# A Mamba-2 + SwiGLU kernel: a new order of its later steps, outputs multiplied in two steps, powers in two passes, the last output bank in two, and four value tiles of block 0 multiplied in three parts

## The chip, the cores and the metric

The kernel runs on one core of one Trainium2 chip. The metric is the device time of one execution in microseconds (us), lower is better. The kernel before has three timed executions: a median of 369.09 us, from 368.76 to 369.15. A separate execution was profiled; it has a time of its own, given below.

A core has a matrix engine (PE in the profile, its weight loads listed apart as PEld), a vector engine (DVE), a scalar engine (ACT), a fourth general engine (POOL) and SP, which here only issues DMA transfers. Each engine works through its own list of instructions in the order of that list and stops at an instruction whose operands are not ready.

## The reference

Two blocks follow each other. The first is a Mamba-2 scan over 4 sequences of 768 tokens with 8 heads of 32 columns and a state of 16; the second is a SwiGLU feed-forward on 3072 tokens of 256 columns, with 1536 hidden columns and an RMS norm ahead of it. All of it is fp32.

```python
# scan, per chunk, batch and head
cum = cumsum(log(a)); L = exp(cum[i] - cum[j]) * causal
M = (C @ B.T) * L
y = M @ x + (C @ state) * exp(cum)
state = exp(sum(log a)) * state + sum_j B_j x_j exp(cum[-1] - cum_j)
# feed-forward on y, as 3072 x 256
xn = y / sqrt(mean(y*y) + 1e-6) * rms_g
g = xn @ w_gate;  val = xn @ w_val
out = (g * sigmoid(g) * val) @ w_out
```

## The kernel before

**Tiling.** Tokens are cut into 12 pairs `p` of 256 tokens for the scan (inside it chunks of 64 tokens) and 6 blocks `blk` of 512 tokens for the feed-forward: block `blk` is made of pairs `2*blk` and `2*blk+1`. The 1536 hidden columns are 12 tiles `f` of 128. For each block and tile there are two products of 512 tokens by 128 columns into a PSUM bank `gv`, gate (`m` = 0) and value (`m` = 1); silu of the gate (ACT, `silu.blk.f`) times the value (DVE, `hid.blk.f`) gives the hidden tile `hx`; and two output products with the out weights add it into the two banks `o` of the block.

**Two ways of multiplying.** A product of fp32 is made in one of two ways. Whole: two plain fp32 matmuls (`F`, `gv_whole`, L1140; `OF`, `o_whole`, L1203). The profile lists each of the two as two records. Split: the operand and the weights are first taken apart into three rounded parts (high, low, mixed) by ACT, DVE and POOL, and six matmuls of the fast rounded type are made, part by part (`X`, `gv_split`, L1150; `OX`, `o_split`, L1197, three matmuls of 512 columns an output bank; in block 5 the same through L1203 as six matmuls of 256 columns). The parts of the normed input `xn` come from steps `xH`/`xHv`, `xL`, `xK`; those of the weights from `wH`/`wHv`, `wL`, `wM`; those of the hidden tile from `hH`/`hHv`, `hL`/`hLp`, `hK`. The names in the profile are `xh`, `xl`, `xk`, `wh`, `wp`, `hh`, `hl`, `hk`. Which way a tile goes is a table: in block 0 tiles 0 and 1 are made early, from unnormed input; tiles 2 to 7 go whole for both gate and value (`GV4`); all else is split. Block 0's outputs all go whole (`O4`).

**Weights.** They arrive as bit words in 18 pieces `k` (two for tiles 0 and 1; 2 to 11 one gate or value half for two tiles each; 12 to 17 the out weights). Each piece is rebuilt on the chip: `pow.k` makes the powers of two on ACT (`power`, three passes over 128x512, L281 to L285, tile `e`), `man.k` the mantissas on DVE (L301), `wt.k` joins them on DVE (L307), and then the three parts follow.

**The scan** of a pair: loads by SP, differences of decays (`spread`, `sub`), exponentials on ACT (`ex`), transposes on DVE (`Tt`, `Td`), additions to the state as products of 64x32 tiles (`A`, L831), the states (`S`, DVE), products of C and B for a block (`gb`, L766), their decays (`L`, DVE), and then the outputs `y.p` (`outputs`, L916): 12 or 16 products of states with `T` and 32 products of chunks with `L`, on 32x64 and 64x32 tiles of PE. They go into four banks for a block; squares (`sq`) and copies (`yt`) by ACT empty them; means (`ms`), roots (`rs`), a broadcast by DMA (`rb`) and `xn` follow.

**The order.** All of it runs under a manual schedule: a string `order` (L1357 on) names 1177 steps, and a loop (L1483) calls each step's function in this order. Each engine's list is the instructions of these steps in that order, so a step moved in the string is moved on every engine that it uses. PSUM has eight banks; `gv`, `o`, `y` and `g` tiles take them in turn, and a bank that is asked for again waits until its last reader is done. ACT's function tables are loaded by hand through `functions` (L259): L264 for silu, L266 for exponentials and logarithms.

**The end.** After the last output products, bank 0 of block 5 is copied by DVE (`putv.5.0`) and bank 1 by ACT (`put.5.1`, L1233), each as one copy of 128x512 followed by two transfers of 128x256 from SP (L1236).

Of the kernel before, what the change touches and what calls it, by code (L numbers as in the profile page):

```python
# [50 lines left out]
def kernel(  # L51
# [222 lines left out]
    def power(k):  # L274
# [15 lines left out]
    def uses_whole(k):  # L290

        if k < 2:
            return 2
        f = 2 * (k // 2) if k < 12 else 2 * (k - 12)
        return sum((gv_mode(blk, g) == 4) if k < 12 else 2 * ((blk, g) in O4)
                   for g in (f, f + 1) for blk in range(NBLK))
# [70 lines left out]
    kinks = const.tile([P, 3], FP32, name="kinks")  # L367
# [60 lines left out]
    def kinks_of_powers():  # L428
        for k, v in enumerate((1152.0, 256.0, -1792.0 * 128.0)):
# [439 lines left out]
    yts, sqs = {}, {}  # L869
# [37 lines left out]
    def outputs(p):  # L907

        n, blk = p % 2, p // 2
        if n == 0:  # L910
            ps["y", blk] = [bank((P, 512), 2, "y") for u in range(4)], set()
        (four, opened), s = ps["y", blk], st[p]

        def product_y(k, u, i, rows, **operands):
            o = four[2 * k + u][1]
            nc.tensor.matmul(out=o[rows, (2 * n + i) * HC:(2 * n + i + 1) * HC],  # L916
                             start=(k, u, rows.start) not in opened, stop=True,
                             skip_group_check=True, **operands)
            opened.add((k, u, rows.start))

        for i in range(2):
            for q in range(NQ):
                for u in range(2):
                    if (2 * p) % NC == 0 and i == 0 and u == 0:
# [3 lines left out]
                    product_y(q // 2, u, i, slice(o, o + 64),  # L928
                              lhsT=S[r].rearrange("p t d -> p (t d)"),
# [3 lines left out]
        opened |= {(k, u, o) for k, u, o_ in opened for o in (o_, o_ + 32)}  # L933
        for i in range(2):
            for hd in range(NH):
                for u in range(2):
                    o = 32 * ((hd + 2 * u) % 4)
                    product_y(hd // 4, u, i, slice(o, o + 32), lhsT=s["x"][halves[u], i, hd],
                              rhs=Ls[p][halves[u], i, hd], tile_position=(HC * u, o))
        s["xb"].used()  # L940
        s["Tb"].used()
# [118 lines left out]
    def modes(blk):  # L1060
        return [gv_mode(blk, f) for f in range(NF)]

    def x_high(blk, t, scaled):
        n = modes(blk).count(3)
        xparts[blk, t, 0] = b = h.take(2 * n + 2, "xh")
# [3 lines left out]
    def x_part(blk, t, i):  # L1069

        xparts[blk, t, i] = b = h.take(2 * modes(blk).count(3), "x" + "hlk"[i])
# [448 lines left out]
```

## Time and profile before

| | |
|---|---|
| median of three timed executions | 369.09 us (368.76 to 369.15) |
| the profiled execution | 368.75 us |
| its span in the trace | 367.0 us |
| PE busy | 360.1 us, 98% of the span, 3293 records |
| DVE busy | 276.7 us, 75%, 514 instructions |
| ACT busy | 203.1 us, 55%, 346 instructions |
| POOL busy | 75.0 us, 20%, 79 instructions |
| granted TensorE clock | 0.998 |

The profiled execution's time is its span and 1.75 us around it. The span is the time from the first to the last instruction of the trace. A busy share is an average over stages: the first 31 us hold the loads and the start of the scan, from then to about 134 us the weights are still being rebuilt while blocks 0 and 1 run, and after that only the scan's and the feed-forward's own work is left. In the lists of groups, a row has the line, the engine, the operation, out<-in with shapes, the count, then busy us and mean ns of one, and behind the second bar the idle time of that engine just before these instructions with what ended it.

### The profile page before, as it was taken

The numbers are of one execution on the slowest core, as the hardware profiler recorded it, in microseconds if no ns is written. First come the engines' busy times: TensorE is split into PE (matmuls) and PEld (weight loads), VectorE is DVE, ScalarE is ACT, GpSimd is POOL, SyncE is SP. The second block draws the span as 40 slices with busy tenths as digits, with TensorE's granted clock in tenths as the row PEclk, the third lists the DMA queues.
The fourth block names the chain that finished last, engine by engine and source line by source line (L and its number), as shares of the span: only waits on it lengthen the run. The fifth ranks groups of instructions, "written<-read, shape, count | busy, mean of one in ns | idle before, by whom it ended". The sixth has DMA issues, their size and how long they took to land.

```text
span 367.0 us, 8226 instructions
## 1 busy us (share of the span) xinstructions
PE 360.1 (98%) x3293; PEld 280.8 (77%) x3293; DVE 276.7 (75%) x514; ACT 203.1 (55%) x346; POOL 75.0 (20%) x79
## 2 busy tenths in 40 slices
PE   8999989999999999999999999999999999999995
PEld 5677455887887777787877778877888888888895
DVE  6899897998998699875867896656447595346790
ACT  3899959999658864486237577034630222421310
POOL 4032010022301311352102316100303001131350
PEclk9999999999999999999999999999999999999999
DMA  7979872564564323542114210110000002001011
GB/s 104 207 136 275 220 292 43 170 143 105 91 120 104 107 47 78 121 63 63 33 30 121 63 29 2 30 30 2 7 29 2 0 10 50 0 0 29 2 30 57
DMA packets 94702, 27.95 MB, mean 76 GB/s; under 512 B 77544, under 2 KB 92616, under 8 KB 94664
## 3 DMA queue, kind: packets, MB, share of 16 engines
q1 hardware_dynamic: 92584, 27.30, 32.6%
q8 instruction: 26, 0.43, 0.5%
q10 hardware_dynamic: 2080, 0.13, 0.4%
q14 instruction: 12, 0.10, 0.1%
HBM read 23.68 MB, written 3.74 MB: 75 GB/s over the span
## 4 chain that ended last, share of the span: by engine, by line
PE 87%; SPq 3%; DVE 3%; ACT 2%; DMA 2%; issue 2%; POOL 0%; ACTq 0%; POOLq 0%; DVEq 0%
PE gv L1150 44%; PE o L1197 18%; PE o L1203 7%; PE gv L1140 4%; PE y L916 3%; PE gv L1105 2%; SPq L186 2%; PE g L766 2%; PE A L831 1%; DMA bq<-in_B_dram 1%; PE g L759 1%; DMA wr<-in_moe_w_out_dram 1%; ACT e L272 1%; SPq L654 1%; PE y L892 1%
## 5 line engine op out<-in xcount | busy, mean ns | idle before, releaser
L272 ACT ACTIVATE hx<-gv 128x512 f32<-128x512 f32 x70 | 40.4, 597 | 90.4 <-PE gv L1150 46.5
L1150 PE MATMUL gv<-xh,wh 128*128 128x512 f32 x256 | 83.0, 405 | 0.0
L1150 PE MATMUL gv<-xl,wp 128*128 128x512 f32 x256 | 79.4, 391 | 0.0
L1150 PE MATMUL gv<-xk,wp 128*128 128x512 f32 x256 | 79.1, 390 | 0.0
L1078 POOL TENSOR_TENSOR hl<-hx,hh 128x512 fp32r<-128x512 f32 x27 | 40.2, 1499 | 150.4 <-PE o L1197 99.5
L1168 DVE SCALAR_TENSOR_TENSOR hx<-gv,hx 128x512 f32<-128x512 f32 x64 | 43.0, 683 | 27.1 <-PE gv L1150 20.6
L1080 DVE SCALAR_TENSOR_TENSOR hk<-hx,hh 128x512 fp32r<-128x512 f32 x60 | 47.5, 810 | 18.6 <-PE o L1197 14.4
L1150 PEld LDWEIGHTS gv<-xl,wp 128*128 128x128 f32 x256 | 48.0, 188 | 10.8 <-DVE xl L1078 0.4
L1150 PEld LDWEIGHTS gv<-xk,wp 128*128 128x128 f32 x256 | 48.0, 188 | 10.4 <-DVE xk L1080 0.2
L1150 PEld LDWEIGHTS gv<-xh,wh 128*128 128x128 f32 x256 | 46.6, 188 | 11.0 <-issue 1.1
L1197 PE MATMUL o<-hh,wh 128*128 128x512 f32 x96 | 37.9, 395 | 0.0
L1197 PE MATMUL o<-hl,wp 128*128 128x512 f32 x96 | 37.4, 389 | 0.0
L1197 PE MATMUL o<-hk,wp 128*128 128x512 f32 x96 | 37.3, 389 | 0.0
L329 ACT ACTIVATE hh<-hx 128x512 fp32r<-128x512 f32 x35 | 21.6, 626 | 25.3 <-PE o L1197 15.8
L1078 DVE TENSOR_TENSOR hl<-hx,hh 128x512 fp32r<-128x512 f32 x33 | 24.1, 729 | 9.9 <-PE o L1197 7.6
L272 ACT ACTIVATE e<-e,kinks 128x512 f32<-128x512 f32 (+1 forms) x36 | 26.0, 722 | 1.2
L323 DVE SCALAR_TENSOR_TENSOR wp<-wh,w 128x512 fp32r<-128x512 f32 x36 | 24.6, 702 | 0.6 <-ACT wh L329 0.5
L632 POOL TENSOR_SCALAR_AFFINE_SELECT L<-L 64x512 f32<-64x512 f32 (+1 forms) x22 | 17.1, 776 | 34.1 <-ACT L L272 32.3
L1203 PE MATMUL o<-w,hx 128*128 128x256 f32 x96 | 23.5, 385 | 0.0
L1140 PE MATMUL gv<-xn,w 128*128 128x512 f32 x48 | 22.4, 603 | 0.0
L266 ACT ACT_TABLE_LOAD x17 | 21.8, 1283 | 1.1 <-PEq L1504 0.8
L1197 PEld LDWEIGHTS o<-hh,wh 128*128 128x128 f32 x96 | 18.0, 188 | 4.1 <-issue 0.2
(173 smaller groups left out, 525.4 us busy)
## 6 DMA issues: line engine op xcount, KB each, us to landing
L<-rowd SPq DMA_DIRECT2D x32, 128.0 KB
x<-in_x_dram SPq DMA_DIRECT2D x24, 128.0 KB
wr<-in_moe_w_out_dram SPq DMA_DIRECT2D x6, 511.5 KB
wr<-in_moe_w_gate_dram SPq DMA_DIRECT2D x5, 511.5 KB
wr<-in_moe_w_val_dram SPq DMA_DIRECT2D x5, 511.5 KB
out_dram<-ob SPq DMA_DIRECT2D x32, 64.0 KB
bc<-in_B_dram SPq DMA_DIRECT2D x23, 64.0 KB
bc<-in_C_dram SPq DMA_DIRECT2D x23, 64.0 KB
```

What stands on the lines that cost most here:

```text
L266: nc.scalar.preload_act_table_set("natural_log_exp_and_others")
L272: nc.scalar.activation(**operands)
L323: nc.vector.scalar_tensor_tensor(out=(low_parts, mixed_parts)[i][k], in0=high_parts[k], scalar=(-UP, GAIN)[i], in1=view(ws[k], shape), op0 ...
L329: nc.scalar.activation(out=out, in_=in_, func=AF.Copy, scale=scale)
L632: nc.gpsimd.affine_select(out=L[r], in_=L[r], pattern=[[0, L.shape[1]], [1, HC]], compare_op=ALU.is_ge, fill=0.0, base=0, channel_multipli ...
L1078: engine.tensor_tensor(out=out, in0=v, in1=high, op=ALU.subtract)
L1080: nc.vector.scalar_tensor_tensor(out=out, in0=v, scalar=REST, in1=high, op0=ALU.mult, op1=ALU.subtract)
L1140: nc.tensor.matmul(out=o, lhsT=view(ws[k], fetched[k][2])[:, t, f % 2 * P:][:, 0:P], rhs=xn[:, t], start=(t == 0), stop=(t == 1))
L1150: nc.tensor.matmul(out=o, lhsT=weights_of(m, t, f)[part], rhs=view(x, [P, TB], F32R), start=(part == t == 0), stop=(part == 2 and t == 1))
L1168: nc.vector.scalar_tensor_tensor(out=v, in0=o, scalar=GAIN, in1=v, op0=ALU.mult, op1=ALU.mult)
L1197: nc.tensor.matmul(out=o, lhsT=w[:, b * P:(b + 1) * P], rhs=v, start=opens, stop=True, skip_group_check=True)
L1203: nc.tensor.matmul(out=o[:, j * DM:(j + 1) * DM], lhsT=v[:, tk], rhs=w, start=opens, stop=True, skip_group_check=True)
```

## The change

Five things are edited.

1. `power` makes the powers with two ACT passes instead of three; its constants `kinks` have two columns instead of three.
2. The table `GV4` is now per gate and value: of block 0's tiles 2 to 7, the value tiles (`m` = 1) of 2, 3, 6 and 7 go split (`X.0.2.1`, `X.0.3.1`, `X.0.6.1`, `X.0.7.1`) instead of whole. The counts of uses follow, and `hide_gv` and `hidden` always use the form with a scalar factor.
3. `outputs` is cut into `outputs_of_states` (step `yi`) and `outputs_of_chunks` (step `ya`), so that other steps may stand between the two.
4. The second output bank of block 5 becomes two half banks: steps `OY.f.j` (`product_apart`, three matmuls of 256 columns each) take the place of `OX.5.f.1`, and `puta.1` and `putva.0` (`put_apart`: one copy of 128x256 and one transfer) that of `put.5.1`.
5. The string `order` is new from its 150th step on (1200 steps now).

```diff
-        activation(out=g, in_=words16, func=AF.Relu, scale=1.0 / 16, bias=kinks[:, 0:1])
-        activation(out=g, in_=g, func=AF.Prelu, scale=-1.0, bias=kinks[:, 1:2],
+        activation(out=g, in_=words16, func=AF.Prelu, scale=-1.0 / 16, bias=kinks[:, 0:1],
                    alpha=2.0 ** -20)
-        activation(out=b16, in_=g, func=AF.Prelu, scale=-2.0 ** 27, bias=kinks[:, 2:3],
+        activation(out=b16, in_=g, func=AF.Prelu, scale=-2.0 ** 27, bias=kinks[:, 1:2],
                    alpha=2.0 ** -20)
...
-        for k, v in enumerate((1152.0, 256.0, -1792.0 * 128.0)):
+        for k, v in enumerate((-896.0, -1792.0 * 128.0)):
...
+    def outputs_of_states(p):
+        s = st[p]
...
+                    product_y(p, q // 2, u, i, o, 64, lhsT=S[r].rearrange("p t d -> p (t d)"),
                               rhs=s["T"][r, i, 3, halves[u]], tile_position=(32 * q, o))
...
+        s["Tb"].used()
+
+    def outputs_of_chunks(p):
+        s, blk = st[p], p // 2
...
+                    product_y(p, hd // 4, u, i, o, 32, lhsT=s["x"][halves[u], i, hd],
                               rhs=Ls[p][halves[u], i, hd], tile_position=(HC * u, o))
...
-    GV4 = {(0, 2), (0, 3), (0, 4), (0, 5), (0, 6), (0, 7)}
+    GV4 = {(0, 2, 0), (0, 3, 0), (0, 4, 0), (0, 4, 1), (0, 5, 0), (0, 5, 1), (0, 6, 0), (0, 7, 0)}
...
-    def gv_mode(blk, f):
-        return 0 if blk == 0 and f < 2 else 4 if (blk, f) in GV4 else 3
+    def gv_mode(blk, f, m):
+        return 0 if blk == 0 and f < 2 else 4 if (blk, f, m) in GV4 else 3
...
+    def gain(blk, f):
+
+        return (GAIN if blk == 0 and gv_mode(blk, f, 1) == 3 else 1.0) * (
+            GAIN if (blk, f) not in O4 else 1.0)
...
-            nc.vector.tensor_tensor(out=v, in0=v, in1=o, op=ALU.mult)
-        else:
-            nc.vector.scalar_tensor_tensor(out=v, in0=o, scalar=GAIN, in1=v, op0=ALU.mult,
-                                           op1=ALU.mult)
+        nc.vector.scalar_tensor_tensor(out=v, in0=o, scalar=gain(blk, f), in1=v, op0=ALU.mult,
+                                       op1=ALU.mult)
...
+    def product_apart(f, j):
+        if j not in apart:
+            apart[j] = bank((P, DM), NF + 1, "o")
+        place, o = apart[j]
+        tk = slice((2 + j) * P, (3 + j) * P)
+        for k, w in enumerate(out_weights_of(f)):
+            v = (hh, hl, hk)[k][NBLK - 1, f]
+            nc.tensor.matmul(out=o, lhsT=view(v, [P, TB], F32R)[:, tk], rhs=w,
+                             start=place.uses == NF + 1 and k == 0, stop=True,
+                             skip_group_check=True)
+            v.used()
+        place.used()
+
+    def put_apart(j, copy):
+        ob = h.take(1, "ob")
+        out_sb = view(ob, [P, DM])
+        place, o = apart[j]
+        copy(out=out_sb, in_=o)
+        rows = slice(T - (2 - j) * P, T - (1 - j) * P)
+        nc.sync.dma_start(out=out[rows], in_=out_sb)
+        ob.used()
+        place.used()
...
-        "A": additions, "S": states, "y": outputs,
+        "A": additions, "S": states, "yi": outputs_of_states, "ya": outputs_of_chunks,
...
+        "OY": product_apart,
+        "puta": lambda j: put_apart(j, ac.copy), "putva": lambda j: put_apart(j, dv.tensor_copy),
...
-        b:OX.5.5.0 b:putv.5.0 b:OX.5.2.1 b:OX.5.1.1 b:put.5.1
+        b:OX.5.6.0 b:OX.5.5.0 b:OY.5.1 b:OY.5.0 b:OX.5.1.0 b:OX.5.2.0 b:OY.4.1 b:OY.2.1
+        b:OY.4.0 b:OY.1.1 b:OY.2.0 b:putv.5.0 b:OY.1.0 b:puta.1 b:putva.0
```

What the new string moves is seen at three places. The first is PE while blocks 1 and 0 overlap: the additions of pairs 6 and 7 (`A`, rows of 32x64) and the means of block 2 (`ms`) between products of 512 columns. Before:

```order
L831 MATMUL A<-x,Bd 32x64 x16
L1150 MATMUL gv<-xh,wh_1485 128x512 x2
L1150 MATMUL gv<-xl,wp 128x512 x2
L1150 MATMUL gv<-xk,wp 128x512 x2
L1150 MATMUL gv<-xh,wh_1169 128x512 x2
L1150 MATMUL gv<-xl,wp 128x512 x2
L1150 MATMUL gv<-xk,wp 128x512 x2
L1012 MATMUL ms<-sq,mean 32x128 x4
```

and with the change:

```order
L1159 MATMUL gv<-xh,wh_998 128x512 x2
L1159 MATMUL gv<-xl,wp 128x512 x2
L1159 MATMUL gv<-xk,wp 128x512 x2
L1234 MATMUL o<-w,hx 128x256 x4
L830 MATMUL A<-x,Bd 32x64 x32
L1014 MATMUL ms<-sq,mean 32x128 x4
L1159 MATMUL gv<-xh,wh_600 128x512 x2
```

Before, the second pair's `A` stood further down by itself; now both pairs' additions and the means are one run of small products. Over the whole program such runs of small products are 29 before (10 with `A`, 9 with `y`, 5 with `ms`, 5 with `g`) and 21 with the change (5, 7, 4 and 5; a run with two kinds is counted once).

The second place is ACT around block 1's squares (`sq`) and copies (`yt`), with powers (`e`) and silu (`hx<-gv`) beside them. Before:

```order
L272 ACTIVATE e<-wr,kinks 128x512
L272 ACTIVATE e<-e,kinks 128x512 x2
L272 ACTIVATE hx<-gv 128x512
L272 ACTIVATE sq<-y 128x4x64 x4
L990 COPY yt<-y 128x4x64
L993 COPY yt<-y 64x4x64 x2
```

and with the change:

```order
L272 ACTIVATE e<-wr,kinks 128x512
L272 ACTIVATE e<-e,kinks 128x512
L328 ACTIVATE wh_825<-w 128x512
L272 ACTIVATE hx<-gv 128x512 x2
L272 ACTIVATE e<-wr,kinks 128x512
L272 ACTIVATE e<-e,kinks 128x512
L992 COPY yt<-y 128x4x64
L995 COPY yt<-y 64x4x64 x2
L272 ACTIVATE sq<-y 128x4x64 x2
```

A power has one row `e<-e` fewer, three powers stand ahead of this piece without a square among them, and the copies now stand ahead of the first squares.

The third place is SP at the program's end, the transfers of the outputs of blocks 4 and 5. Before:

```order
L1229 DMA out_dram<-ob 32x16x32 x8
L1030 DMA roots_3539<-roots 128x128
L1037 DMA r<-roots_3539 32x4x128 x4
L1229 DMA out_dram<-ob 32x16x32 x16
L1236 DMA out_dram<-ob 128x256 x4
```

and with the change:

```order
L1260 DMA out_dram<-ob 32x16x32 x8
L1032 DMA roots_3649<-roots 128x128
L1039 DMA r<-roots_3649 32x4x128 x4
L1260 DMA out_dram<-ob 32x16x32 x16
L1267 DMA out_dram<-ob 128x256 x2
L1218 DMA out_dram<-ob 128x256 x2
```

There are as many transfers as before; the last two now belong to two copies, and only one of them to the last.

On ACT the change has 33 + 5 = 38 loads of a function table instead of 33; up to the products of block 3 (`gb.3`) there are 13 in both. On PE it has 16 plain fp32 matmuls of gate and value tiles instead of 24, and 792 split ones instead of 768; the output products in block 5 are 144 in both.

More of the change, by code (lines that the diff above doesn't have):

```diff
@@ L905, in first_outputs, with outputs_of, product_y @@
         s["Tb"].used()
[L907 to L919, printed above, removed]
+    def outputs_of(p):
+        if p // 2 not in yparts:
+            yparts[p // 2] = [bank((P, 512), 2, "y") for u in range(4)], set()
+            ps["y", p // 2] = yparts[p // 2]
+        return yparts[p // 2]
+    def product_y(p, k, u, i, first, n, **operands):
+        four, opened = outputs_of(p)
+        groups = {(k, u, r) for r in range(first, first + n, 32)}
+        o = four[2 * k + u][1]
+        nc.tensor.matmul(out=o[first:first + n, (p % 2 * 2 + i) * HC:(p % 2 * 2 + i + 1) * HC],
+                         start=not groups & opened, stop=True, skip_group_check=True, **operands)
+        opened |= groups
+    def outputs_of_states(p):
+        s = st[p]
         for i in range(2):
@@ L1114, in normed @@
         us[0, f] = h.take(2, "u")
-        hx[0, f] = h.take(2, "hx")
+        hx[0, f] = h.take(2 if (0, f) in O4 else 3, "hx")
         r = ps["r", 0]
@@ L1130, in hidden @@
         ub = us.pop((0, f))
-        nc.vector.tensor_tensor(out=v, in0=view(ub, [P, TB]), in1=v, op=ALU.mult)
+        nc.vector.scalar_tensor_tensor(out=v, in0=view(ub, [P, TB]),
+                                       scalar=1.0 if (0, f) in O4 else GAIN, in1=v,
+                                       op0=ALU.mult, op1=ALU.mult)
         ub.used()
```

249 lines of the change are left out of this document (123 added, 126 removed).

## The prediction

> **What bounds the kernel now.** I read the page first: the span, the busy times, and the share of each engine in the chain of waits that ended last.
>
> ```profile
> span 367.0 us, 8226 instructions
> PE 360.1 (98%) x3293; PEld 280.8 (77%) x3293; DVE 276.7 (75%) x514; ACT 203.1 (55%) x346; POOL 75.0 (20%) x79
> PE 87%; SPq 3%; DVE 3%; ACT 2%; DMA 2%; issue 2%; POOL 0%; ACTq 0%; POOLq 0%; DVEq 0%
> ```
>
> PE is 98% busy and 87% of the chain; nothing else has more than 3%. A busy share hides the stages, so the view of windows comes next: the span's start, the stage in which the weights are rebuilt (31.4 to 133.4, where block 3's products are reached), and a late piece. Columns: length, then PE, PEld, DVE, ACT and POOL busy with counts, clock, DMA share, GB/s.
>
> ```profile
> 0.00:31.40 31.40, 29.77 (x361) 21.09 (x362) 26.43 (x74) 24.06 (x51) 9.87 (x24) 1.00 0.87 174
> 31.40:133.40 102.00, 100.92 (x1059) 71.64 (x1065) 92.01 (x183) 85.33 (x140) 16.68 (x17) 1.00 0.55 138
> 280.00:300.00 20.00, 20.00 (x90) 16.57 (x89) 15.32 (x28) 3.55 (x6) 1.61 (x1) 1.00 0.00 0
> ```
>
> In the middle stage PE stands still for about 1 us of 102, but DVE is idle for only 102.00 − 92.01 = 10.0 us and ACT for 16.7. So PE sets the time, with DVE close behind it until 133 us; later DVE has room (15.32 of 20). What PE's work is made of stands in the chain of waits:
>
> ```profile
> 35.36 7.06 PE gv L1140 x16
> 312.49 5.44 PE gv L1150 x24
> 347.29 15.84 PE o L1203 x132
> 363.23 0.59 ACT ob L1233
> ```
>
> A whole tile is four records, so 7.06 / 4 = 1.77 us; a split tile six, so 5.44 / 24 × 6 = 1.36 us. Block 5's outputs run at 15.84 / 132 = 0.12 us a matmul of 256 columns, and behind the last stands only ACT's copy and the transfer. Every microsecond taken from PE's list after 31.4 us is then worth one at the end, as long as DVE does not come up to it.
>
> **The change part by part.** *Four value tiles split.* 4 × (1.77 − 1.36) = −1.64 us on PE. The whole rows include what it costs to come from another kind of product ahead of them, so the lower bound of the gain is some −1.3. I take **−1.5**. DVE's multiply behind them costs the same in either form, as its two groups show:
>
> ```profile
> L1166 DVE TENSOR_TENSOR hx<-hx,gv 128x512 f32<-128x512 f32 x6 | 4.0, 680 | 0.0
> L1168 DVE SCALAR_TENSOR_TENSOR hx<-gv,hx 128x512 f32<-128x512 f32 x64 | 43.0, 683 | 27.1 <-PE gv L1150 20.6
> ```
>
> *Runs of small products.* The new order has 21 runs of small products on PE where there were 29, with the same small products in them. What does a run cost beyond its products? The timeline of PE shows one of `A` between an output product and a split tile; the view of windows with that stretch cut up tells how many of its 24 records were in flight.
>
> ```profile
> 164.74 0.39 PE L1197 MATMUL o<-hk,wp 128*128 128x512 f32 x1
> 165.06 0.43 PE L831 MATMUL A<-x,Bd 64*32 64x64 f32 x24
> 165.42 0.50 PE L1150 MATMUL gv<-xh,wh 128*128 128x512 f32 x1
> 165.13:165.21 0.08, 0.08 (x19) 1.00 0.00 0
> 165.21:165.29 0.08, 0.08 (x24) 1.00 0.00 0
> ```
>
> From the one wide product to the next are 165.42 − 164.74 = 0.68 us, where two wide ones alone stand 0.23 apart: the run costs 0.45. Its small products are all under way by 165.29, that is within 0.23 of their start at 165.06, so 0.22 to 0.45 belongs to going there and back. Nineteen were under way after 0.15, so I take the smaller share for the products and 0.32 for the way. 8 × 0.32 = −2.6. Inside the remaining runs the kind of small product changes three times more often; no row isolates such a change, it lies between 0 and a whole run's way, and I take 0.15 each, +0.4. Sum **−2.2**, bounds −1.8 + 1.0 = −0.8 and −3.6.
>
> *Outputs in two steps.* PE once stands inside `y`, in this group:
>
> ```profile
> L916 PE MATMUL y<-L,x 64*32 64x64 f32 x640 | 9.1, 224 | 1.3 <-issue 1.3
> ```
>
> The wait of 1.3 us is named only as issue. With the states' and chunks' products apart it could go (−1.3) or stay; for pairs 2 and 3 nothing of PE is put between the halves, so I take 0.
>
> *The last bank.* Rows of the end and the nearest copies of 256 columns:
>
> ```profile
> 361.79 0.69 DVE L1233 COPY ob<-o 128x512 f32<-128x512 f32 x1 [3.88 <-PE o L1203]
> 362.51 2.14 SPq L1236 DMA_DIRECT2D out_dram<-ob  x4
> L698 DVE COPY T<-tp 128x256 f32<-128x256 f32 x1 | 0.4, 414 | 0.0
> ```
>
> Today ACT copies 512 columns in 0.59 and SP issues two transfers behind it, four in 2.14, so 0.54 each. With the change a copy of 0.41 on DVE and one transfer remain: −0.18 − 0.54 = −0.7 if issuing is all that counts, −0.2 if SP is still busy with the transfers of `puta`. I take **−0.6**.
>
> *Two passes for powers.* ACT's groups in the window from 30 to 134 us:
>
> ```profile
> L272 ACT ACTIVATE e<-wr,kinks 128x512 f32<-128x512 int16 x14 | 10.7, 761 | 0.0
> L272 ACT ACTIVATE e<-e,kinks 128x512 f32<-128x512 f32 x14 | 10.1, 723 | 0.5
> L272 ACT ACTIVATE e<-e,kinks 128x512 int16<-128x512 f32 x14 | 10.1, 722 | 0.5
> L264 ACT ACT_TABLE_LOAD x7 | 9.0, 1283 | 0.1
> ```
>
> One pass goes: 18 × 0.72 = −13.0 us of ACT, 10.1 of them here (85.3 busy becomes 75), against 5 more table loads × 1.28 = +6.4, none of these before block 3's products. ACT is not on the path, so this is **0** by itself, hidden behind PE; where that cover is thin is the start: 4 powers there, at most 2.9 us, but the first 149 steps keep their order and there DMA (share 0.87) and PE's 29.77 of 31.40 lie beside them, so I take 0 for it too. What it does buy is fewer waits of DVE for ACT:
>
> ```profile
> DVE w L307 <- ACT e L272: 2.8, 3, 2.2
> DVE A L848 <- PE A L831: 1.9, 2, 1.0
> DVE hk L1080 <- ACT hh L329: 1.6, 1, 1.6
> DVE hx L1168 <- ACT hx L272: 1.0, 1, 1.0
> DVE T L193 <- DMA bq<-in_B_dram: 1.0, 1, 1.0
> DVE wp L323 <- ACT wh L329: 0.5, 1, 0.5
> DVE T L193 <- DMA bc<-in_C_dram: 0.4, 1, 0.4
> ```
>
> (waits of DVE in the same window: us, times, longest). The longest, 2.2, comes from ACT standing at block 1's squares with two powers queued behind them:
>
> ```profile
> 52.39 1.21 ACT L272 ACTIVATE sq<-y 128x256 f32<-128x256 f32 x4 [3.77 <-PE y L916]
> ```
>
> In the new order three powers stand ahead of that place and only copies follow PE there.
>
> *What is late next: DVE.* Ahead of block 3's products the new order has nine DVE instructions that came later before (six parts of weights or hidden tiles, decays, a transpose and a product of the hidden) and three fewer, six more net. Their nearest row is
>
> ```profile
> L323 DVE SCALAR_TENSOR_TENSOR wp<-wh,w 128x512 fp32r<-128x512 f32 x32 | 21.2, 682 | 0.6 <-ACT wh L329 0.5
> ```
>
> so at most 6 × 0.68 = 4.1; some are on 256 columns, and I take 3. PE has less ahead of it there: −1.5 for the split tiles, one split tile moved behind it (−1.36) and three runs (−1.0), 3.8 us in all. PE then comes after 102.0 − 3.8 = 98.2 us, and DVE needs 92.0 + 3 = 95.0 and its waits: at most 3.2 us of idle may remain. If the waits on ACT go (2.8 + 1.6 + 1.0 + 0.5 = 5.9), 10.0 − 5.9 = 4.1 remains, and PE would wait 0.9; with some of ACT's left I take **+1.1**, bounds 0 and, with all 10 us of idle kept, 10.0 − 3.2 = +6.8.
>
> Sum: 368.75 − 1.5 − 2.2 − 0.6 + 1.1 = 365.55 for the profiled execution. That one ran 0.34 under the median of the three, so **365.9 us** is predicted for the median.
>
> [...]
>
> **The rivals.** *First: DVE becomes the bound of the middle stage (slower).* Place: the vector instructions ahead of block 3's products. If the waits on ACT are replaced by others, since every step has a new neighbour, the idle stays at 10 us and PE waits 6.8: 368.75 − 4.3 + 6.8 = 371.25, 371.6 at the median. It is slower than before from the point where DVE's idle exceeds 3.2 + 4.3 = 7.5 us. For it: there are pieces of this stage in which DVE and ACT both hardly pause, as in this row of the windows:
>
> ```profile
> 60.00:70.00 10.00, 10.00 (x42) 7.57 (x41) 9.71 (x20) 9.71 (x16) 0.00 (x0) 1.00 0.40 116
> ```
>
> Against it: 13 us less on ACT. In between, with an idle of 5.5 to 7.5, stands a **second**, partial case: 367.4 to 369.1, middle 368.2.
>
> *Third: PE's list is not what counts.* If the way to small products is hidden and the gain of the four split tiles is waited away at their operands, which DVE and ACT must now make earlier, only the end is gained: 368.75 − 0.6 = 368.15, 368.5 at the median. For it: split tiles need six parts ready, whole ones none, and the four now stand at the front of block 0's split tiles. Against it: the run above, which costs 0.45 in the trace with PE never waiting for data.
>
> *Fourth: the start is shortened too.* If the four early powers lie on the path of the first whole tiles, up to 2.9 us go there; half of it gives 365.9 − 1.5 = 364.4. Against it: DMA's 0.87 in that stage.
>
> **How the numbers follow.** Forecast 0.55, its own range 364.0 to 367.3 (a PE wait of 0 to 2.2, the runs' bounds on the other side). First rival 0.15, second 0.14, third 0.07, fourth 0.09. Three executions of the kernel before spread over 0.39 us, so I call 0.2%, 0.74 us, the least that a measurement tells from no change: same is 368.35 to 369.83. Faster: forecast and fourth, 0.64, and two thirds of the second, 0.09, less what the forecast's own tail gives away: 0.72. Same: the third and the rest of the second, 0.13. Slower: the first, 0.15. The range that leaves out 2 in 10 goes from 363.2 (fourth, nearly all of it) to 369.4 (second and third inside, the first outside).
>
> **What would show it.** In the changed kernel's profile: ACT's `e<-e,kinks` at 18 instead of 36 and its busy time near 203.1 − 6.6 = 196; split groups at L1159 264 a part; PE's gap around a run of small products still 0.45; DVE's list of waits from 30 to 134 us without the 2.2 at `e`; the last copy on DVE at 0.41 with one transfer behind it; PE reaching block 3's products 2 to 4 us earlier. I am wrong if PE shows waits of more than 2 us in total for operands made by DVE between 60 and 130 us, if the end from the last matmul on is not shorter, or if the runs of small products cost less by their number than 0.22 each.

## The result, and the profile after

The changed kernel takes **374.92 us** (median of five, 374.23 to 375.49), the kernel before 368.83 in the runs beside it: a ratio of 1.016 with an interval of 1.0146 to 1.0174, slower by 6.1 us, where 365.9 us was forecast, 2.9 us faster. The profiled execution took 374.38 us, near its median.

The page of the changed kernel, the same three rows as before the change:

```profile
span 372.5 us, 8234 instructions
PE 361.0 (97%) x3301; PEld 285.4 (77%) x3301; DVE 275.6 (74%) x514; ACT 197.4 (53%) x333; POOL 72.5 (19%) x79
PE 86%; DVE 6%; DMA 3%; issue 2%; SPq 2%; POOL 1%; DVEq 0%; POOLq 0%
```

Hardly anything moves here: PE is still nearly always busy, and its busy time grew by 0.9 us while the span grew by 5.5. The share of the chain says more: DVE has 6% and DMA 3% where they had 3% and 2%. The list of PE's waits (us in total, times, longest) names the places:

```profile
PE ms L1014 <- POOL sq L974: 3.1, 1, 3.1
PE y L916 <- issue: 2.0, 1, 2.0
PE gv L1159 <- DVE L L788: 0.8, 1, 0.8
PE gv L1159 <- DVE xl L1080: 0.4, 1, 0.4
PE gv L1159 <- DVE hx L1174: 0.2, 1, 0.2
PE o L1234 <- DVE hk L1082: 0.2, 1, 0.2
PE gv L1159 <- DVE xk L1082: 0.2, 1, 0.2
```

The largest is one wait of PE for POOL, an engine that is busy for 19% of the span. How it came about stands in the chain of waits of the changed kernel, 52 to 69 us (start, length, what; SPq is the issuing of transfers on SP):

```profile
52.80 0.51 SPq L653
...
53.35 7.70 DMA L<-rowd
...
61.21 1.05 POOL L L659
62.26 1.68 POOL sq L974
...
63.98 0.42 PE ms L1014 x8
64.40 2.73 PE gv L1159 x6
67.14 1.31 PE o L1234 x4
```

It is to be read from the bottom: the means of block 1 (`ms`) waited for the sum of its squares on POOL (`sq`); on POOL that sum stood behind a subtraction of block 2's decays (`L`, step `subp.10`); and the subtraction waited 7.70 us for a load. Why the load took so long was not tried; SP had issued three transfers of weights just ahead of it (at 49.44 us), and in the windows of 52 to 56 and 56 to 60 us the share of the DMA engines reads 1.01 and 1.07. In the kernel before, POOL's timeline has the sum first and a subtraction of such a load only 18 us behind it:

```profile
53.74 2.13 POOL L972 TENSOR_TENSOR sq<-sq 128x512 f32<-128x512 f32 x1 [21.73 <-ACT sq L272]
73.41 1.04 POOL L660 TENSOR_TENSOR L<-L,tok 128x512 f32<-128x512 f32 x1 [17.54 <-DMA L<-rowd]
```

The last two rows of the chain hold a second loss: six split matmuls took 2.73 us instead of 1.36, and four whole ones of the outputs 1.31, where such rows elsewhere in this chain have 0.86. The windows with the granted clock (the third column from the right) say why:

```profile
64.00:67.00 3.00, 3.00 (x15) 2.23 (x16) 3.00 (x6) 2.94 (x5) 0.81 (x1) 0.58 0.62 221
67.00:70.00 3.00, 3.00 (x13) 2.48 (x12) 2.21 (x4) 2.94 (x6) 0.23 (x1) 0.85 0.16 51
```

Behind the pause PE ran at half clock for about (0.42 + 0.15) x 3 x 2 = 3.4 us (cut at 64.50, 67.00 and 67.90 us, the windows read a clock of 0.50 in both pieces), which by the clock costs 3.4 / 2 = 1.7; the two slow rows took (2.73 − 1.36) + (1.31 − 0.86) = 1.8 us more.

DVE's waits in the same kernel, 30 to 134 us, changed as a whole:

```profile
DVE hk L1082 <- DMA out_dram<-ob: 4.8, 1, 4.8
...
DVE w L306 <- ACT e L272: 0.8, 1, 0.8
```

The waits for ACT's powers fell from 2.8 to 0.8 us as forecast, but one wait of 4.8 us stands in their place: a part of a hidden tile needed the place from which block 0's output was still being sent. So DVE's idle time in the middle stage is 102.00 − 92.27 = 9.7 us, as large as before:

```profile
31.40:133.40 102.00, 96.52 (x1036) 72.58 (x1035) 92.27 (x180) 73.51 (x123) 18.00 (x18) 0.98 0.55 138
```

ACT's powers have 14 + 14 passes in this window (42 before), the split groups 264 matmuls a part, and the end is shorter, as the last chain rows show:

```profile
367.17 2.17 PE o L1206 x18
369.34 0.02 issue
369.37 0.42 DVE ob L1216
```

From PE's last product to the end of the span are 372.5 − 369.34 = 3.2 us, before 367.0 − 363.13 = 3.9.

### The profile page after: what moved, and what is told of

The parts are those of the page before. It is cut to its first block, busy times and chain, and to the rows that moved or that the text cites. A ratio compares the mean times of both kernels' runs of the same rounds, so it can differ in the third digit from the quotient of the medians.

```text
span 372.5 us, 8234 instructions
## 1 busy us (share of the span) xinstructions
PE 361.0 (97%) x3301; PEld 285.4 (77%) x3301; DVE 275.6 (74%) x514; ACT 197.4 (53%) x333; POOL 72.5 (19%) x79
## 4 chain that ended last, share of the span: by engine, by line
PE 86%; DVE 6%; DMA 3%; issue 2%; SPq 2%; POOL 1%; DVEq 0%; POOLq 0%
PE gv L1159 44%; PE o L1228 17%; PE o L1234 6%; PE gv L1149 4%; PE y L916 2%; DMA L<-rowd 2%; PE gv L1112 2%; PE o L1206 2%; PE g L765 2%; PE A L830 1%; PE g L758 1%; DVE hk L1082 1%; PE e L595 1%; SPq L173 1%; DMA x<-in_x_dram 1%
## 5 line engine op out<-in xcount | busy, mean ns | idle before, releaser
L1159 PE MATMUL gv<-xh,wh 128*128 128x512 f32 x264 | 85.9, 407 | 1.1 <-DVE L L788 0.8
L1159 PE MATMUL gv<-xl,wp 128*128 128x512 f32 x264 | 82.1, 392 | 0.4 <-DVE xl L1080 0.4
L1159 PE MATMUL gv<-xk,wp 128*128 128x512 f32 x264 | 82.0, 392 | 0.2 <-DVE xk L1082 0.2
L1080 POOL TENSOR_TENSOR hl<-hx,hh 128x512 fp32r<-128x512 f32 x27 | 38.1, 1414 | 181.1 <-PE o L1228 85.6
L1174 DVE SCALAR_TENSOR_TENSOR hx<-gv,hx 128x512 f32<-128x512 f32 x70 | 47.0, 682 | 25.8 <-PE gv L1159 24.8
L1159 PEld LDWEIGHTS gv<-xl,wp 128*128 128x128 f32 x264 | 49.8, 189 | 11.5 <-DVE xl L1080 0.8
L1159 PEld LDWEIGHTS gv<-xk,wp 128*128 128x128 f32 x264 | 49.8, 189 | 11.3 <-DVE xk L1082 0.7
L1159 PEld LDWEIGHTS gv<-xh,wh 128*128 128x128 f32 x264 | 48.5, 188 | 13.0 <-issue 1.3
L322 DVE SCALAR_TENSOR_TENSOR wp<-wh,w 128x512 fp32r<-128x512 f32 x36 | 28.0, 804 | 0.6 <-ACT wh L328 0.6
L1234 PEld LDWEIGHTS o<-w,hx 128*128 128x128 f32 x96 | 18.3, 194 | 4.2 <-DVE w L306 0.5
```

The lines of the kernel that those rows point to most:

```text
L322: nc.vector.scalar_tensor_tensor(out=(low_parts, mixed_parts)[i][k], in0=high_parts[k], scalar=(-UP, GAIN)[i], in1=view(ws[k], shape), op0 ...
L1080: engine.tensor_tensor(out=out, in0=v, in1=high, op=ALU.subtract)
L1159: nc.tensor.matmul(out=o, lhsT=weights_of(m, t, f)[part], rhs=view(x, [P, TB], F32R), start=(part == t == 0), stop=(part == 2 and t == 1))
L1174: nc.vector.scalar_tensor_tensor(out=v, in0=o, scalar=gain(blk, f), in1=v, op0=ALU.mult, op1=ALU.mult)
L1234: nc.tensor.matmul(out=o[:, j * DM:(j + 1) * DM], lhsT=v[:, tk], rhs=w, start=opens, stop=True, skip_group_check=True)
```

## The experiments

Times are medians of 9 to 12 executions beside the kernel before (368.7 to 369.0 in these runs), unless said otherwise. Single executions of one kernel mostly lie within 3.4 us of each other, so the intervals are given.

**POOL's order.** *squares_first* moves one word of the order:

```diff
-        b:OF.0.0.1 b:sq.1.0 p:subp.10 p:spread.11 i:pow.14 b:X.0.3.1 b:X.0.2.1 i:wH.9 b:X.0.9.0
-        b:X.0.8.0 b:sqa.1 i:wt.7
+        b:OF.0.0.1 b:sq.1.0 p:spread.11 i:pow.14 b:X.0.3.1 b:X.0.2.1 i:wH.9 b:X.0.9.0
+        b:X.0.8.0 b:sqa.1 p:subp.10 i:wt.7
```

> The changed kernel with one step moved: POOL's subtraction of group 10 (subp.10) stands behind the sum of block 1's squares (sqa.1), no longer ahead of it. Theory 1 (POOL's order: the sum stood behind a subtraction whose load lands late, PE waited 3.1 us for it and then ran 3.4 us at half clock, 1.7 us of work): the PE wait at ms.1 goes to under 0.5 us, the half-clock stretch at 64 us goes, and the time falls by 4 to 5 us to 370.0 to 371. Rival A (the sum is late because ACT's squares or PE's outputs are late): the wait stays over 2 us and the time over 373. Rival B (PE would wait for something else there in any case): the wait moves to another operand within 10 us and the time falls by less than 2 us. PE's list is the same as in the changed kernel: if the pause of 2.0 us seven products before the end of pair 5's outputs is one of instruction delivery it stays at the same product; if it is a wait for data it moves or goes, because PE arrives 4 us earlier.

Measured: 370.22 us, ratio 1.0043 (1.0022 to 1.0064). 4.7 of the 6.1 us are gone. POOL's timeline in this kernel:

```profile
55.53 2.35 POOL L974 TENSOR_TENSOR sq<-sq 128x512 f32<-128x512 f32 x1 [23.29 <-DVE wh L331]
60.75 1.16 POOL L659 TENSOR_TENSOR L<-L,tok 128x512 f32<-128x512 f32 x1 [2.86 <-DMA L<-rowd]
```

The sum is made 6.7 us earlier, before the load lands, PE has no wait at the means, and the clock stays at 1.00 in the profiled execution. What is left of PE's waits:

```profile
PE y L916 <- issue: 1.7, 1, 1.7
PE o L1234 <- DVE w L306: 1.3, 2, 0.8
PE gv L1159 <- DVE L L788: 0.8, 1, 0.8
```

*subtract_first_in_before* goes the other way, from the kernel before: a load of decays is issued earlier, and its subtraction moves from DVE to POOL, ahead of the sum.

```diff
-        b:F.0.4.1 p:y.3 b:silu.0.4 ... b:F.0.2.1 b:sqa.1 ... p:spread.8 ... p:sub.8
+        b:F.0.4.1 p:y.3 p:spread.8 b:silu.0.4 ... b:F.0.2.1 p:subp.8 b:sqa.1
```

> The kernel before with the cause of theory 1 put into it: block 2's first load of decays (spread.8) is issued right behind pair 3's outputs, and its subtraction goes to POOL (subp.8) ahead of the sum of block 1's squares. Theory 1: the load lands 4 to 8 us after its issue at about 52.5 us, so the sum comes 3 to 7 us later than at 53.7 us and PE waits 1 to 5 us at ms.1 (57.8 us); if the wait is over 3 us, a stretch of half clock follows it. Time 370 to 375. Rivals A and B: PE's wait at ms.1 stays under 0.5 us and the time is 368.8 within 0.7.

Measured: 370.09, ratio 1.0045 (1.0024 to 1.0065), and the same wait appears:

```profile
PE ms L1012 <- POOL sq L972: 2.5, 1, 2.5
```

The load landed 3.84 us after its issue, the wait is 2.5 us, and in the profiled execution no half clock followed it: the clock reads 1.00 from 59.2 to 65 us. The 3 us of wait that the expectation asks for is the author's estimate from the one wait of the changed kernel, 3.1 us with a half clock behind it. The time rose by less than the wait, by 1.2 us; in this profile the pause of 1.0 us that the kernel before has inside pair 2's outputs is missing, which makes up for part of it. That the order on POOL makes PE wait is shown from both sides; that it is worth 4.7 us in the changed kernel is shown by squares_first.

**A pause of 2.5 us and one of 3.1.** *longer_pause_in_before* puts two more transfers and a weight piece (`p:qc.5`, `i:fetch.9`) ahead of `p:spread.8` in the kernel just told; it was run once. The subtraction's load is then issued 2.7 us later (54.26 against 51.59 us).

> As subtract_first_in_before, where PE stood 2.5 us at block 1's means and no stretch of half clock followed, with two more transfers and a weight piece ahead of the load that the subtraction waits for. Theory 5 (a PE pause of some 3 us or more is followed by some 3.4 us at half clock): the pause grows to 3.5 to 6 us, and right behind it the granted clock is about 0.5 for 3 to 4 us. Rival (the half clock in the changed kernel had another cause): the pause grows and the clock stays at 1.00. The time is that of the kernel before and 2 to 6 us.

Measured: 374.28 us. Theory 5's 3 us and 3.4 us are those of the changed kernel's one pause (3.1 us, then 3.4 at half clock). PE's wait grew to 3.1 us, from 57.89 to 60.95, and the windows read:

```profile
58.00:60.00 2.00, 0.00 (x0) 0.00 (x0) 2.00 (x3) 1.93 (x5) 1.96 (x2) 1.00 0.00 0
60.00:60.90 0.90, 0.00 (x0) 0.00 (x0) 0.90 (x1) 0.88 (x2) 0.90 (x1) 0.50 0.00 0
58.00:60.90 2.90, 0.00 (x0) 0.00 (x0) 2.90 (x3) 2.81 (x6) 2.85 (x2) 0.84 0.00 0
61.00:64.00 3.00, 3.00 (x11) 1.33 (x12) 3.00 (x7) 2.70 (x6) 0.00 (x0) 0.50 0.07 22
64.00:67.00 3.00, 3.00 (x7) 1.87 (x6) 1.66 (x4) 2.94 (x5) 0.00 (x0) 0.53 0.59 185
```

The clock was at half for (0.16 x 2.9 + 0.50 x 3.0 + 0.47 x 3.0) x 2 = 6.7 us. The first two rows show when it fell: at 60.0 us, still inside the pause and 2.1 us after PE's last product had ended. So some 5.9 us of it lie on work and cost 2.9. With a pause only 0.6 us longer, this one execution took 4.7 us more than the profiled one of the run before (369.61), of which 0.6 for the pause, 2.9 for the half clock and 0.95 for the pause inside pair 2's outputs, which is back in this profile. The size of the pause was under the 3.5 to 6 us expected, the half clock longer than the 3 to 4.

**The pause inside the outputs.** In the changed kernel PE stands 2 us ahead of the last seven products of pair 5, with nothing named:

```profile
110.52 0.49 PE L916 MATMUL y<-T,S 32*64 32x64 f32 x32
110.93 0.79 PE L916 MATMUL y<-L,x 64*32 64x64 f32 x57
113.72 0.31 PE L916 MATMUL y<-L,x 64*32 64x64 f32 x7 [1.99 <-issue]
```

In squares_first PE came there 4 us earlier and stood ahead of the same product:

```profile
109.62 0.31 PE L916 MATMUL y<-L,x 64*32 64x64 f32 x7 [1.66 <-issue]
```

*squares_first_outputs_apart* puts wide products between the two pairs' outputs:

```diff
-        b:X.1.6.1 ... b:OF.0.9.1 p:dT.9 p:yi.4 p:ya.4 i:wL.13 p:x.7 p:vB.11 p:yi.5 p:ya.5
+        ... p:dT.9 p:yi.4 p:ya.4 i:wL.13 p:x.7 p:vB.11 b:X.1.6.1 b:OF.0.9.1 p:yi.5 p:ya.5
```

> As squares_first, and two steps of wide products (X.1.6.1 and OF.0.9.1, 2.2 us of PE) moved from ahead of pair 4's outputs to between pair 4's and pair 5's. Theory 2 (a run of 320 small products outruns the delivery of PE's instructions): the pause in pair 5's outputs goes from 2.0 to under 0.7 us, one more run of small products costs 0.3 to 0.45, and the time is 1 to 1.7 us under squares_first. Rival (the pause is a wait for an operand of pair 5): the time of the start of pair 5's last products does not change and the time is that of squares_first within 0.5 us.

Measured: 369.51, ratio 1.0026 (1.0003 to 1.0048). The pause is gone from pair 5. In its place 0.5 us of waits stand at pair 4, which now comes earlier. The gain over squares_first is 0.7 us, less than the 1 to 1.7 expected.

*squares_first_values_whole* (below) has eight records fewer on PE ahead of this place, and there the pause stood eight records further on, inside the next output product:

```profile
107.55 0.86 PE L916 MATMUL y<-L,x 64*32 64x64 f32 x64
108.34 0.48 PE L1234 MATMUL o<-w,hx 128*128 128x256 f32 x1
109.77 1.78 PE L1234 MATMUL o<-w,hx 128*128 128x256 f32 x7 [0.94 <-issue]
```

Counted in the traces, it is ahead of PE's 1233rd record in all three kernels. So the pause belongs to a place in PE's list, not to an operand, and it shows when a run of some 185 small products (32 + 64 + 32 + 57; the expectation's 320 is not the right count) stands just ahead of that place. The length of the run is not all of it: in the kernel before, the outputs of pairs 4 and 5 are one run of 192 without a pause, and its pause of 1.0 us stands ahead of record 599, behind 85 small products. Nor is the size of the pause fixed: seven profiles with that same old list up to there have from 0 to 1.2 us at record 599. What causes it was not shown: that instructions are delivered too slowly there, as theory 2 has it, is the author's guess, and the profile has no row for their delivery to PE.

**The parts alone, in the old order.** *two_passes_in_before* has edit 1 only, *last_bank_in_two_in_before* edit 4 only, and *old_order_all_but_values* the changed code with the old order and whole value tiles.

```diff
-        activation(out=g, in_=words16, func=AF.Relu, scale=1.0 / 16, bias=kinks[:, 0:1])
-        activation(out=g, in_=g, func=AF.Prelu, scale=-1.0, bias=kinks[:, 1:2],
+        activation(out=g, in_=words16, func=AF.Prelu, scale=-1.0 / 16, bias=kinks[:, 0:1],
...
```

> The kernel before with the powers made in two passes, nothing else. The prediction's term: ACT has 13 us less to do, none of it on the path, so 0 us (368.8 within 0.5). Rival (the four early powers lie on the path of the first whole tiles): 1 to 2.9 us faster, and PE comes to the first whole tile, 32.3 us before, at 30 to 31.5 us.

Measured: 368.89, ratio 1.0001 (0.9985 to 1.0017). DVE's wait for the powers fell from 2.8 to 0.6 us, and nothing came of it at the end, as forecast.

```diff
...
-        b:OX.5.2.1 b:OX.5.1.1 b:put.5.1
+        b:OY.2.0 b:OY.2.1 b:OY.1.1 b:puta.1 b:OY.1.0 b:putva.0
```

(the other products of the second bank, `OX.5.f.1`, are likewise two steps `OY.f.0` and `OY.f.1` at the same places)

> The kernel before with the last output bank in two, nothing else. The prediction's term: 0.6 us faster (bounds 0.2 to 0.9), 368.2, and the stretch from PE's last product to the end of the span shrinks from 3.9 to about 3.2 us. Rival (SP is still busy with the transfers ahead, or the transfer's landing sets the end): no change within 0.3 us.

Measured: 369.26, ratio 1.0004 (0.9984 to 1.0024): no gain that can be told. In its profile PE's last product ends at 363.00 and the span at 366.6, 3.6 us, 0.3 less than before; the last two transfers are issued from 363.32 to 364.23, where before the four took until 364.65 (362.51 + 2.14).

> The changed kernel's code with the order of the kernel before, and all of block 0's value tiles 2 to 7 whole as before: two-pass powers, the outputs' two halves still one behind the other, the last bank in two. If what made the change slow is the order, this is 0.4 to 0.9 us faster than the kernel before (368.0 to 368.4). If it is one of the other parts, it is slower than 369.5.

Measured: 368.62, ratio 0.9986 (0.9970 to 1.0002). In the old order edits 1, 3 and 4 are harmless; what made the kernel slow is in the new order and in edit 2.

**Runs of small products.** *runs_of_additions_apart* cuts four runs of squares_first_values_whole in two, *old_order_additions_merged* takes two away from old_order_all_but_values.

```diff
-        b:table.1 p:A.6 p:dT.6 ... p:A.7 b:ms.2 ... b:X.1.7.0 ... b:X.1.9.1
+        b:table.1 p:A.6 p:dT.6 ... b:X.1.7.0 p:A.7 b:X.1.9.1 b:ms.2
```

(and `b:X.2.7.0` between `p:A.9` and `p:A.8`, `b:OX.2.3.0` between `p:A.10` and `p:A.11`)

> As squares_first_values_whole (369.0), with four runs of small products cut in two by a step of wide products that stood right behind them (pairs 6 and 7, the means of block 2, pairs 8 and 9, pairs 10 and 11): 25 runs instead of 21. The prediction's term: 0.32 us a run (0.22 to 0.45), so 1.3 us slower, 370.3. The changed kernel's own trace puts a run at 0.25, so 1.0 slower. Rival (the way to small products is hidden behind other waits): no change within 0.4 us.

Measured: 371.90 (four runs), ratio 1.0088 (1.0065 to 1.0111), 2.9 us over squares_first_values_whole, more than twice what was expected. One of the new runs in its timeline:

```profile
118.83 0.63 PE L1159 MATMUL gv<-xk,wp 128*128 128x512 f32 x2
119.39 0.45 PE L830 MATMUL A<-x,Bd 64*32 64x64 f32 x32
119.78 0.73 PE L1159 MATMUL gv<-xh,wh 128*128 128x512 f32 x2
```

From the wide product ahead to the one behind the run are 119.78 − 118.83 − 2 x 0.23 = 0.49 us, of which 32 small products at 0.007 take 0.22: 0.27 for the way. Four of them are 1.1 us. Of the other 1.8 the profile has 1.3 in waits that squares_first_values_whole does not have (0.8 us for block 3's decays, 0.5 for `w`); the moved wide products shifted what stands ahead of them.

```diff
-        p:A.4 ... p:qb.9 p:A.5 ... p:A.6 ... p:S.6 ... p:A.7
+        p:A.4 p:A.5 ... p:qb.9 ... p:A.6 p:A.7 p:S.6
```

> As old_order_all_but_values (368.6), with the additions of pairs 4 and 5 put together and those of pairs 6 and 7: two runs of small products fewer. 0.5 us faster by the trace's 0.25 a run, 368.1, which would be faster than the kernel before by 0.2%. Rival (pair 5's operand is not ready at the earlier place, or the states of pair 6 come too late): PE waits there and the time stays at 368.6 or grows.

Measured: 369.92, ratio 1.0034 (1.0020 to 1.0049): slower by 1.3 us, the rival. Between PE's records two runs fewer saved 0.5 us, but DVE then stood for the later addition, and PE for DVE (the first row is of DVE's waits, the others of PE's):

```profile
DVE A L847 <- PE A L830: 4.3, 2, 3.3
```

```profile
PE y L916 <- issue: 1.7, 2, 0.9
PE gv L1159 <- DVE A L847: 0.6, 1, 0.6
```

The pauses named issue are 1.1 us more than in the profile of old_order_all_but_values (0.6). As they vary from profile to profile, only the wait of 0.6 is shown to come from the merging.

**The four value tiles.** *squares_first_values_whole* makes them whole again at the same places, *outputs_apart_values_whole* does so behind squares_first_outputs_apart.

```diff
-    GV4 = {(0, 2, 0), (0, 3, 0), (0, 4, 0), (0, 4, 1), (0, 5, 0), (0, 5, 1), (0, 6, 0), (0, 7, 0)}
+    GV4 = {(0, f, m) for f in range(2, 8) for m in range(2)}
...
-        b:X.0.3.1 b:X.0.2.1 ... b:X.0.7.1 ... b:X.0.6.1
+        b:F.0.3.1 b:F.0.2.1 ... b:F.0.7.1 ... b:F.0.6.1
```

> As squares_first, with block 0's value tiles 2, 3, 6 and 7 multiplied whole again at the places where the change has them split. The prediction's term: PE has 4 x 0.36 to 0.41 us more to do, so 1.3 to 1.6 us slower than squares_first (370.2), near 371.6. Rival (the split tiles wait for their parts and give the gain back): the same time as squares_first within 0.5 us.

> As squares_first_outputs_apart (369.5), with the four value tiles whole again. Theory 4 (PE has caught up with DVE in this order, so a shorter list of PE before block 3's products only turns into waits, and the split tiles bring nothing): within 0.5 us of 369.5 or faster, PE's waits for DVE before 140 us shrink by about the 1.3 us that PE's list grows. Rival 1 (the split tiles save their 1.3 us of PE, and squares_first_values_whole was faster only because PE's pause of instruction delivery fell behind pair 5's outputs): 370.5 to 371. Rival 2 (what made squares_first_values_whole faster is neither): under 368.5.

Measured: 369.01, ratio 1.0001 (0.9983 to 1.0020), so 1.2 us faster than split; and 370.62, ratio 1.0047 (1.0027 to 1.0067), so 1.1 us slower than split. Since these contradict each other and were measured on different chips, all four kernels ran again on one chip.

> The kernel of squares_first again, beside the next three on one chip. If split tiles save what PE saves and the pause in pair 5's outputs costs what it holds up, this is slower than split_two_runs by 0.7 to 1.5 us and about as fast as whole_one_run (370.2 against 369 to 370). The pause stands ahead of the same product as before, seven before the end of pair 5.

> The kernel of squares_first_values_whole again. Theory 4 (DVE binds before 140 us, the split tiles bring nothing): equal to or faster than split_one_run, by up to 1.2 us. Rival (the split tiles save 1.3 us): 0.5 to 1.5 us slower than split_one_run.

> The kernel of squares_first_outputs_apart again: pair 5's outputs apart, no pause. 369.5 by the first measurement.

> The kernel of outputs_apart_values_whole again. Theory 4: within 0.5 us of split_two_runs or faster. Rival (the split tiles save 1.3 us where no pause hides it): 0.8 to 1.5 us slower than split_two_runs. If both pairs come out with the same sign, the first measurements were scatter between chips or executions.

| | outputs of pairs 4 and 5 in one run | apart |
|---|---|---|
| split | 370.31 (1.0017 to 1.0052) | 369.57 (0.9996 to 1.0022) |
| whole | 368.88 (0.9981 to 1.0008) | 370.72 (1.0023 to 1.0059) |

In brackets the interval of the ratio to the kernel before. All four came out within 0.13 us of the first time: it is not scatter between chips. In the upper left five of the twelve executions had a mean clock of 0.995, the others 0.999 or more; without the five its median is 370.0, so a half clock does not set it apart. The split tiles save 1.2 us where the outputs are apart and cost 1.4 where they are in one run. In the upper left the pause falls inside pair 5's outputs; its second profile has DVE waiting 4.0 us for the transfer of block 0's output, which stands on SP behind the next loads of decays (in the changed kernel they are issued from 114.21 us, the transfer at 118.00), and PE 0.8 us for block 3's decays. In the lower left the pause falls just behind those outputs, and neither of its profiles has either wait. That the pause leads to these waits is read from the order and not tried by itself. Why the lower right is slow is open: its two profiles fell on faster executions (368.15 and 369.68 us) and show no wait that would make it.

**The place that DVE waited for.** *squares_first_outputs_apart_put_later* moves one step further:

```diff
-        i:wM.13 b:put.0.1 p:qb.6 ... b:hK.1.0 b:hK.1.10 b:yt.2.0
+        i:wM.13 p:qb.6 ... b:hK.1.0 b:hK.1.10 b:put.0.1 b:yt.2.0
```

> As squares_first_outputs_apart, and the copy and transfers of block 0's second output bank (put.0.1) stand behind the two mixed parts hK.1.0 and hK.1.10, so that no part of a hidden tile has to wait for the place that the transfer reads from. Theory 3 (DVE's longest idle time, 4.8 us in the changed kernel and 2.8 in squares_first_outputs_apart, is that wait, and it makes DVE late for block 3's products): that idle time goes, PE's waits for block 3's decays and for pair 7's operands (0.8 us in the changed kernel) go under 0.2, and the time falls by 0.3 to 1 us against squares_first_outputs_apart (369.5). Rival (DVE is late there because of its own work): the idle time moves to other instructions before 140 us and the time stays within 0.3 us.

Measured: 370.08, ratio 1.0026 (1.0011 to 1.0041). The rival held. The wait for the transfer, 2.8 us in squares_first_outputs_apart, went from DVE's list, others took its place, and PE waited 0.8 us for block 3's decays as in squares_first (the same row as there). So that wait of PE does not hang on DVE's wait for the transfer alone. New in DVE's list are

```profile
DVE L L659 <- PE A L830: 2.1, 1, 2.1
DVE T L193 <- DMA bc<-in_C_dram: 1.8, 1, 1.8
```

## Why the prediction was wrong

**The step that failed** is "what is late next". It looked for the next late engine in DVE alone, and never at POOL's list. The squares of block 1 were mentioned as ACT's; that their sum is made by POOL, and what now stands ahead of it there, was not asked. POOL's list would have told: with the change a subtraction of decays stands ahead of the sum of squares, and before it stood behind. Its load is issued at 52.8 us and lands 7.70 later. That is 4.7 of the 9.0 us between forecast and result: about 3.1 of wait and 1.7 of half clock. Of the rest the profile holds 0.85 us at the start, 0.7 in the pause inside the outputs (2.0 against 1.3), 0.7 in waits for DVE (1.8 in the rows above against the sum's 1.1), 0.8 in what the runs of small products gave less than expected, and 0.85 in the wide products: counted from start to start and without the half clock they take 0.65 us less than before, where 1.5 was taken for the split tiles. Some 0.4 us is not traced.

None of the prediction's three signs of being wrong came up in the changed kernel: PE's waits for DVE between 60 and 130 us stay far under 2 us, the end is shorter, and the eight runs of small products fewer saved 0.25 us each. All three signs looked where the sum had looked.

**The half clock** was in no term and in no rival. The prediction priced a wait at its length; this one of 3.1 us cost 1.7 more. What sets a pause's price is not its length alone, as the last section shows.

**DVE as the bound (first rival)** had the sign, and its time of 371.6 lies between squares_first and the changed kernel, but its mechanism is not what happened: of DVE's 9.7 us of idle time in the changed kernel 4.8 are one wait for a transfer's place, not new neighbours everywhere, and in squares_first, which still has that wait (4.7), only 102.00 − 95.54 = 6.5 us are left in the same window, under the 7.5 from which this rival made the kernel slower. Block 3's products, forecast 2 to 4 us earlier, start 3.0 us later in the changed kernel and 1.1 us earlier in squares_first. Their rows in the timelines of the kernel before, the changed one and squares_first:

```profile
133.12 1.21 PE L766 MATMUL g<-T 32*64 32x128 f32 x64
136.15 1.25 PE L765 MATMUL g<-T 32*64 32x128 f32 x64
132.06 1.23 PE L765 MATMUL g<-T 32*64 32x128 f32 x64
```

The wait of +1.1 us for DVE that the sum held is 0.8 at block 3's decays and 1.3 at `w` in squares_first.

**The four split value tiles**, taken at −1.5: in the four pairs of profiles with and without them PE's wide products, from start to start, take 0.8 to 1.7 us less, and the result is −1.2 in one setting and +1.4 in the other. The step treated a shorter list as time saved; here the eight records more on PE also put a pause of PE into the middle of pair 5's outputs.

**Runs of small products**, taken at 0.32 each: 0.27 by the row above and 0.24 in the merged kernel, within the bounds of 0.22 to 0.45. In the changed kernel the eight runs fewer saved 2.0 us between PE's records, and three more changes inside runs, with a wider spacing there, took back some 0.6, so −1.4 in place of −2.2. That a merged run needs its operands earlier, or makes their readers later, was left out, and in the old order that cost PE a wait of 0.6 us, as much as the two runs saved.

**The outputs in two steps**, taken at 0 with a possible gain of 1.3: the pauses did not go. The one at pair 2 (1.0 us) is not in the changed kernel's profile, one of 2.0 us at pair 5 is.

**The last bank**, taken at −0.6: the end of the changed kernel is 0.7 us shorter. Alone in the old order it was 0.3 in one profile and nothing in the medians.

**The powers**, taken at 0: 0 with an interval from −0.6 to +0.6 us. Here the mechanism was as told, down to DVE's wait for them.

**The start.** The first whole tile came 0.85 us later in the changed kernel's profile (33.35 against 32.50 in the chains) with the same list ahead of it. In the profiles of the other kernels it is spread over the same range, so this is not counted as the change's.

With the order mended, the changed kernel is at 368.9 to 370.3 depending on edit 2, and no version here is faster than the kernel before beyond its interval; the nearest is old_order_all_but_values (0.9970 to 1.0002).

## What to carry to other kernels

When an order is changed, read the list of every engine that the moved steps touch, the idle ones first: an engine that is 19% busy held up the busiest one for 3.1 us here, because something short that was waited for (1.68 us) stood behind something that waited 7.70 us for a load. Price a long wait of PE with the half clock that can follow it: behind the 3.1 us of the changed kernel it was 3.4 us, worth 1.7. A shorter list on the bounding engine need not be time saved (the four split tiles here: −1.2 us in one setting, +1.4 in the other): see whether what it feeds and what feeds it keep their places, change one of these at a time, and measure pairs of edits together, since here two edits of 1 us each had opposite signs with and without each other.

## What the runs showed of the hardware

In the profiled executions a PE pause of 2.5 us (subtract_first_in_before) left the granted clock at 1.00, and pauses of 3.1 us came with 3.4 us (the changed kernel) and 6.7 us (longer_pause_in_before) at half clock. The length of the pause does not decide alone: in longer_pause_in_before the clock fell 2.1 us after the modelled end of PE's last product, inside the pause, and in the changed kernel at about 64.5 us (67 − 0.42 x 3 x 2), half a microsecond after PE had resumed at 63.98. What sets when the clock falls and for how long was not shown. Two of the changed kernel's five executions had a mean clock of 0.991, the other three 0.994 or 0.995; that is by estimate 0.0035 x 373 x 2 = 2.6 us more at half clock with the same instructions. And one of the ten executions of subtract_first_in_before had 0.995 where the others have 0.997 or more, and was the longest with 372.75 us, so a half clock may have followed the shorter pause there too.

A pause of 0.9 to 2.0 us on PE sat ahead of the same place of its list, the 1233rd record, in all six profiles of the new order with the outputs of pairs 4 and 5 in one run, with different operands there, and in none of the five with two steps of wide products put into that run.
